# Issue order of the first loads, place of a query chunk, load slots, and the split of query transposes between DMA and PE

## The chip, the cores and the metric

The kernel runs on one core of a Trainium2 chip. The time is device microseconds (us) of that core, over several executions; the profile is of one of them. TensorE is PE, VectorE DVE, ScalarE ACT, GpSimd POOL, SyncE SP; PEclk is the share of PE's clock that was granted. On one core, slow is a run more than 1.5% above the fastest of the same kernel. A ratio's bracket is its 95% interval. Ratios are the mean time of one kernel's fast runs over that of the other's of the same rounds, so they are not quite the ratio of the medians that are quoted.

## The reference

Linear attention with cosine features, then a feed-forward network (FFN) with a product of two projections. Cut to what matters:

```python
def _attn_ref(q, k, v):                       # q, k, v: 8 batches x 8 heads x 576 x 64
    theta = np.pi / 2.0 * np.arange(S) / S
    phi = lambda x: concat([relu(x) * cos(theta), relu(x) * sin(theta)])   # 64 -> 128 features
    kv = einsum('bhsf,bhsd->bhfd', phi(k), v)
    z = sum(phi(k), axis=2)
    num = einsum('bhsf,bhfd->bhsd', phi(q), kv)
    den = einsum('bhsf,bhf->bhs', phi(q), z)[..., None] + 1e-06
    return num / den

def _moe_ref(x, w1, w2, w3, w_out):           # x: 4608 x 512, inner width 1024
    return (x @ w1) * (x @ w2) @ w3 @ w_out
```

Inputs and output are float32.

## The kernel before

W3 and w_out are multiplied into one matrix (w34b) at run time. The attention of a later batch is woven into the slots of each FFN tile, so that PE always has matmuls. The attention output (xblk) is turned into FFN input (xT) by PE for batch 0 and by DMA transposes from SP for all later batches. In the views, kf is the first keys in f32; ks, qs and vs are keys, queries and values in bf16; kp and qp are their features, qpT the turned query features and pst the buffer that PE turns them into; ffnps holds an FFN product and osb an output that is ready to be stored. Cuts are marked with dots:

```python
    load(0, "k", nc.sync)                     # first keys, f32, by SP's DMA queue
    load(0, "q")                              # bf16 (cast in the DMA), by GpSimd's queue
    ...
    idle_mms(32)                              # matmuls on zeros, before the keys land
    cosv, sinv = _trig_tables(nc, const)      # starts with two iotas on GpSimd
    identb = const.tile([P, P], BF16, name="identb")
    make_identity(nc, identb[:])
    ...
    load(0, "v")
    ...                                       # weights, then k, v, q of batch 1
    load(2, "kqv")

    def dma_q(b):                             # query chunks that a DMA turns, not PE
        return [] if b < 2 else order_of(b)[2:] if b < B - 1 else order_of(b)

    def features(dst, src, c):                # one chunk: cosine half on DVE, sine half on ACT
        ...

    def x_tr(b, c):                           # a chunk of attention output into xT, FFN's input
        ...
        if b >= 1:
            nc.sync.dma_start_transpose(out=xT[t][:, :, ds(o, R)], in_=xf)
            return
        ...                                   # batch 0: by PE, copied by ACT

    for t in range(NT):                       # nine FFN tiles of 512 rows, 24 slots each
        slots = [[] for _ in range(24)]
        if t == 0:
            ...
            attention_at(1, between, ..., nu=(12, 14, 16, 18, 20), xt=(12, 14, 16, 18, 20))
            ...
            slots[16].append(lambda: load(3, "kqv"))
            spread(prep_units(2), 17, 23, slots)
        else:
            if t + 3 < B:
                for g, name in ((0, "k"), (4, "q"), (8, "v")):
                    slots[g].append(lambda name=name: load(t + 3, name))
            ...
```

Of the kernel before, what the change touches and what calls it, by code (L numbers as in the profile page):

```python
# [19 lines left out]
NCH = 5  # L20
# [3 lines left out]
def _trig_tables(nc, pool):  # L24

    s_i = pool.tile([P, NCH], I32, name="s_i")
    nc.gpsimd.iota(s_i[0:64, :], pattern=[[1, 5]], base=0, channel_multiplier=5)
    nc.gpsimd.iota(s_i[64:128, :], pattern=[[1, 5]], base=320, channel_multiplier=4)
    th = pool.tile([P, NCH], FP32, name="th")
    nc.vector.tensor_copy(out=th[:], in_=s_i[:])  # L30
    nc.vector.tensor_scalar_mul(out=th[:], in0=th[:], scalar1=math.pi / 2 / S)
    t2 = pool.tile([P, NCH], FP32, name="t2")
    nc.vector.tensor_mul(out=t2[:], in0=th[:], in1=th[:])

    def poly(outt, coefs):
        nc.vector.tensor_scalar_mul(out=outt[:], in0=t2[:], scalar1=float(coefs[0]))
        for c in coefs[1:-1]:
            nc.vector.scalar_tensor_tensor(out=outt[:], in0=outt[:], scalar=float(c), in1=t2[:],
                                           op0=ALU.add, op1=ALU.mult)

    cosv = pool.tile([P, NCH], FP32, name="cosv")
    poly(cosv, [-1 / 3628800, 1 / 40320, -1 / 720, 1 / 24, -1 / 2, 1.0])
    nc.vector.tensor_scalar_add(out=cosv[:], in0=cosv[:], scalar1=1.0)
    sinv = pool.tile([P, NCH], FP32, name="sinv")
    poly(sinv, [-1 / 39916800, 1 / 362880, -1 / 5040, 1 / 120, -1 / 6, 1.0])
    nc.vector.scalar_tensor_tensor(out=sinv[:], in0=sinv[:], scalar=1.0, in1=th[:],
                                   op0=ALU.add, op1=ALU.mult)
    return cosv, sinv
# [3 lines left out]
def kernel(  # L52
# [12 lines left out]
    B = q.shape[0]  # L65
# [23 lines left out]
    def load(b, which, eng=nc.gpsimd):  # L89
        for name in which:  # L90
            src = {"k": k, "v": v, "q": q}[name]
            if eng is nc.gpsimd:
                t = ld.tile([P, H, NCH, D], BF16, name=name + "s")
            else:
                t = wst.tile([P, H, NCH, D], FP32, name=name + "f", bufs=1)
            eng.dma_start(out=t[0:64, :, :, :].rearrange("p h j d -> p h (j d)"),  # L96
                                in_=src[b, :, 0:320, :].rearrange("h (p j) d -> p h (j d)", j=5))
            eng.dma_start(out=t[64:128, :, 0:4, :].rearrange("p h j d -> p h (j d)"),
                                in_=src[b, :, 320:S, :].rearrange("h (p j) d -> p h (j d)", j=4))
            raw[b, name] = t  # L100
# [10 lines left out]
        nc.gpsimd.dma_start(out=w3b[:, jp, :], in_=moe_w3[ts(jp, P), :])  # L111

    load(0, "k", nc.sync)
    load(0, "q")
    zeros = const.tile([P, 512], BF16, name="zeros")
    nc.vector.memset(zeros[:], 0.0)
    tiny = const.tile([P, 1], FP32, name="tiny")
# [4 lines left out]
    def idle_mms(n):  # L122

        for _ in range(n):
            nc.tensor.matmul(unread[:, :], lhsT=zeros[:, 0:128], rhs=zeros[:], start=True, stop=True)

    idle_mms(32)
    cosv, sinv = _trig_tables(nc, const)
    identb = const.tile([P, P], BF16, name="identb")
    make_identity(nc, identb[:])  # L130
    va_bufs = []
    for i in range(2):
        va = const.tile([P, NCH, H, D + 2], BF16, name=f"va{i}")
# [42 lines left out]
    def order_of(b):  # L176

        return [0, 1, 2, 3, 4] if b % 2 == 0 else [4, 0, 1, 2, 3]

    def dma_q(b):  # L180

        return [] if b < 2 else order_of(b)[2:] if b < B - 1 else order_of(b)

    feat = {}

    def feat_of(b):
        if b not in feat:
            feat[b] = (
                phi.tile([P, NCH, H, F], BF16, name="kp"),
                phi.tile([P, NCH, H, F], BF16, name="qp"),  # L190
                va_bufs[b % 2],
            )
        return feat[b]
# [8 lines left out]
    def features(dst, src, c):  # L202
        R = ROWS[c]
        nc.vector.tensor_scalar(out=dst[:R, c, :, 0:D], in0=src[:R, :, c, :], scalar1=0.0,  # L204
                                scalar2=cosv[:R, c:c + 1], op0=ALU.max, op1=ALU.mult)
        nc.scalar.activation(out=dst[:R, c, :, D:F], in_=src[:R, :, c, :], func=ACTF.Relu,  # L206
                             scale=sinv[:R, c:c + 1], bias=0.0)

    def prep_k(b, c):
        features(feat_of(b)[0], raw[b, "k"], c)  # L210

    def prep_q(b, c):
        features(feat_of(b)[1], raw[b, "q"], c)
        if c in dma_q(b):
            R = ROWS[c]
            nc.sync.dma_start_transpose(out=att_of(b)["qpT"][:, :, ds(128 * c, R)],
                                        in_=feat[b][1][:R, c].rearrange("p h f -> p (h f)"))
# [42 lines left out]
    def q_tr(b, c, evac=True):  # L260
        R = ROWS[c]
        qp = feat[b][1]
        pst = ps_tr.tile([P, 8, 128], BF16, name="pst")
        for h in range(H):
            nc.tensor.transpose(pst[:, h, 0:R], qp[:R, c, h, :], identb[:R, :R])  # L265
        dst, src = att_of(b)["qpT"][:, :, ds(128 * c, R)], pst[:, :, 0:R]
        on_vector = lambda: nc.vector.tensor_copy(out=dst, in_=src)  # L267
        on_scalar = lambda: nc.scalar.copy(out=dst, in_=src)  # L268
        if evac:
            on_vector()  # L270
        return on_vector, on_scalar
# [22 lines left out]
    def x_tr(b, c):  # L294
        R = ROWS[c]
        xblk = att[b]["x"].pop(c)
        xf = xblk[:R].rearrange("p g h d -> p (g h d)")
        if b % 2 == 0:
            slot = S * b + 128 * c
        else:  # L300
            slot = S * b + (0 if c == 4 else 64 + 128 * c)
        t, o = divmod(slot, 512)
        if t not in xT:
            xT[t] = xtp.tile([P, 4, 512], BF16, name="xT")
# [3 lines that stand above are left out]
        pst = ps_tr.tile([P, 8, 128], BF16, name="pst")  # L308
        for kc in range(4):
            nc.tensor.transpose(pst[:, kc, 0:R], xf[:, ts(kc, 128)], identb[:R, :R])  # L310
        nc.scalar.copy(out=xT[t][:, :, ds(o, R)], in_=pst[:, 0:4, 0:R])
# [101 lines left out]

    for c in range(NCH):
        prep_k(0, c)
    for c in range(NCH):
        prep_q(0, c)
    q_tr(0, 0)
    q_tr(0, 1)
    idle_mms(1)  # L420
    for c in range(NCH):
        prep_v(0, c)
    for c in (2, 3):
        q_tr(0, c, evac=False)[1]()
    kv_first()
    idle_mms(1)
    num(0, 0)
# [10 lines left out]
    for t in range(NT):  # L438
        slots = [[] for _ in range(24)]
        if t == 0:  # L440
            slots[0].append(lambda: x_tr(0, 2))
            slots[1].append(lambda: x_tr(0, 3))
            slots[4].append(lambda: q_tr(0, 4))
            slots[7].append(lambda: num(0, 4))
            slots[9].append(lambda: x_tr(0, 4))
            slots[14].append(lambda: w3_tr(0))
            between = [[] for _ in range(32)]
            spread(prep_units(1, (prep_k,)), 2, 4, between)
            spread(prep_units(1, (prep_v,)), 5, 7, between)
            spread(prep_units(1, (prep_q,)), 8, 11, between)  # L450
            attention_at(1, between, kv=(7, 8, 8, 9, 9), tr=(10, 11, 13, 15, 17),
                         nu=(12, 14, 16, 18, 20), xt=(12, 14, 16, 18, 20))
            for jp in range(8):
                for part in range(2):
                    if part == 0 and jp < 7:
                        slots[15].append(lambda jp=jp: w3_tr(jp + 1))
                    slots[15].append(lambda jp=jp, part=part: w34_mm(jp, part))
                    slots[15] += between[2 * jp + part]
            for g in range(16, 24):
                slots[g] += between[g]  # L460
            slots[16].append(lambda: load(3, "kqv"))
            spread(prep_units(2), 17, 23, slots)
        else:
            if t + 3 < B:
                for g, name in ((0, "k"), (4, "q"), (8, "v")):
                    slots[g].append(lambda name=name: load(t + 3, name))
            if t + 1 < B:
                attention_at(t + 1, slots, kv=(0, 1, 2, 3, 4), tr=(2, 4, 7, 10, 13),
                             nu=(6, 8, 11, 14, 17), xt=(6, 8, 11, 14, 17))
            if t + 2 < B:  # L470
                each = [u for c in zip(*(prep_units(t + 2)[i:i + NCH] for i in (0, 5, 10))) for u in c]
                spread(each, 0, 22, slots)
        for g, _ in enumerate(ffn_groups(t)):
            for u in slots[g]:
                u()
# [30 lines left out]
```

## Time and profile before

| | before |
|---|---|
| median of the first three runs | 265.04 us (264.79 to 272.18, the last one slow) |
| span of the profiled run | 264.2 us |
| PE busy | 248.9 us, 94% |
| second keys land, first FFN matmul | 11.04 us, 24.20 us |
| FFN tile 1 starts, tile 2 starts | 69.75 us, 95.82 us |
| DMA transposes issued from SP | 55 (35 of xT, 20 of qpT) |

PE is nearly always busy, so a change helps only where it shortens PE's own work or removes one of its waits. The prediction below shows the lines from which I read that.

### The profile page before, as it was taken

What the parts mean: (1) busy time and instruction counts of PE and PEld (TensorE: products, weight loads), DVE (VectorE), ACT (ScalarE), POOL (GpSimd) and SP (SyncE); (2) the same over time, 40 slices, a digit from 0 to 9 for tenths busy, and PEclk for the clock granted to TensorE, in tenths of its full rate; (3) what the DMA queues carried; (4) which work ended last, traced back from release to release, by engine and by line L of the source; (5) the groups of instructions that cost most, each with busy time, mean ns of one, the idle gap of its engine ahead of it and who ended that gap; (6) DMA issues with size and microseconds to landing.
All of it is one profiled execution on the core that took longest, in us unless ns stands there. A gap on an engine that the chain in (4) does not pass through costs nothing.

```text
span 264.2 us, 4955 instructions
## 1 busy us (share of the span) xinstructions
PE 248.9 (94%) x1874; PEld 131.6 (50%) x1907; DVE 139.1 (53%) x334; ACT 125.6 (48%) x214; POOL 84.7 (32%) x143
## 2 busy tenths in 40 slices
PE   8478999999999989999999999999999999999993
PEld 3166545665464435445544545464445444444442
DVE  4366447567879616863883387278615723412320
ACT  2393435554955545555554565546543224333322
POOL 7552244331592275027504740430050022013000
PEclk9979999999999999999999999999999999999999
DMA  7999999999999999999997899744880334005014
GB/s 131 222 198 207 210 201 203 200 198 193 165 180 166 163 213 169 188 176 195 173 195 150 161 187 154 161 101 81 120 188 22 51 80 121 0 16 143 4 40 120
DMA packets 70600, 38.61 MB, mean 146 GB/s; under 512 B 38192, under 2 KB 67120, under 8 KB 70576
## 3 DMA queue, kind: packets, MB, share of 16 engines
q0 software_dynamic: 32400, 27.20, 63.2%
q1 hardware_dynamic: 38016, 10.95, 28.0%
q8 instruction: 15, 0.25, 0.4%
q10 hardware_dynamic: 160, 0.13, 0.2%
q14 instruction: 9, 0.07, 0.1%
HBM read 38.80 MB, written 9.44 MB: 183 GB/s over the span
## 4 chain that ended last, share of the span: by engine, by line
PE 85%; DMA 7%; ACT 3%; DVE 1%; issue 1%; SPq 0%; ACTq 0%
PE ffnps L353 47%; PE ffnps L382 20%; PE ffnps L170 5%; PE pnum L231 4%; DMA xT<-xblk 4%; PE pnum L281 4%; DMA kf<-in_k_dram 4%; PE pst L265 4%; PE pst L158 1%; ACT kp L206 1%; DVE xblk L288 1%; ACT qpT L268 1%; PE ffnps L399 0%; SPq L96 0%; ACT osb L401 0%
## 5 line engine op out<-in xcount | busy, mean ns | idle before, releaser
L377 DVE TENSOR_TENSOR abT<-asb,ffnps 128x512 bf16<-128x512 bf16 x70 | 47.9, 684 | 72.3 <-PE ffnps L353 71.2
L353 PE MATMUL ffnps<-xT,w1b 128*128 128x512 bf16 (+1 forms) x307 | 74.7, 362 | 2.3 <-DMA xT<-xblk 1.3
L353 PE MATMUL ffnps<-xT,w2b 128*128 128x512 bf16 (+1 forms) x296 | 73.2, 362 | 0.7
L373 ACT CAST asb<-ffnps 128x512 bf16<-128x512 f32 x70 | 40.9, 585 | 67.3 <-PE ffnps L353 61.7
L382 PE MATMUL ffnps<-w34b,abT 128*128 128x512 bf16 x273 | 63.2, 379 | 0.4
L345 POOL DMA_DIRECT2D out_dram<-osb x44 | 23.5, 540 | 121.9 <-ACT osb L388 121.8
L353 PEld LDWEIGHTS <-w1b 128*128 128x128 bf16 x312 | 27.9, 98 | 30.8 <-issue 3.0
L382 PEld LDWEIGHTS <-abT 128*128 128x128 bf16 x280 | 26.7, 98 | 30.6
L353 PEld LDWEIGHTS <-w2b 128*128 128x128 bf16 x312 | 26.8, 98 | 24.6
L388 ACT COPY osb<-ffnps 128x512 f32<-128x512 f32 x35 | 20.4, 584 | 38.6 <-PE ffnps L382 36.6
L206 ACT ACTIVATE qp<-qs,sinv 128x512 bf16<-128x512 bf16 (+1 forms) x40 | 28.0, 718 | 0.0
L288 DVE TENSOR_TENSOR xblk<-pnum,den 128x512 bf16<-128x512 f32 (+1 forms) x38 | 26.2, 689 | 1.5 <-DVE den L286 0.2
L206 ACT ACTIVATE kp<-ks,sinv 128x512 bf16<-128x512 bf16 (+1 forms) x35 | 24.5, 721 | 0.0
L281 PEld LDWEIGHTS <-qpT 128*128 128x128 bf16 (+1 forms) x320 | 14.9, 100 | 11.6 <-issue 3.6
L222 POOL COPY va<-vs 128x512 bf16<-128x512 bf16 (+1 forms) x30 | 18.8, 655 | 0.0
L265 PE MATMUL pst<-identb,qp 128*128 128x128 bf16 (+1 forms) x160 | 12.2, 226 | 5.3 <-ACT qp L206 5.3
L281 PE MATMUL pnum<-kvs,qpT 128*128 128x65 bf16 (+1 forms) x304 | 16.2, 194 | 0.0
L204 DVE TENSOR_SCALAR qp<-qs,cosv 128x512 bf16<-128x512 bf16 (+1 forms) x40 | 16.0, 418 | 0.0
L265 PEld LDWEIGHTS <-qp 128*128 128x128 bf16 (+1 forms) x160 | 10.4, 104 | 10.6 <-ACT qp L206 5.8
L231 PEld LDWEIGHTS <-kp 128*128 128x128 bf16 (+1 forms) x280 | 12.3, 97 | 6.6 <-issue 1.7
L170 PE MATMUL ffnps<-woutb,w3T 128*128 128x512 bf16 x60 | 15.2, 379 | 0.2
L267 DVE COPY qpT<-pst 128x1024 bf16<-128x1024 bf16 (+1 forms) x18 | 11.3, 630 | 7.4 <-PE pst L265 7.2
(64 smaller groups left out, 163.7 us busy)
## 6 DMA issues: line engine op xcount, KB each, us to landing
out_dram<-osb POOLq DMA_DIRECT2D x20, 256.0 KB, 3.9
out_dram<-osb POOLq DMA_DIRECT2D x24, 128.0 KB, 3.4
qs<-in_q_dram POOLq DMA_DIRECT2D x8, 320.0 KB, 9.2
vs<-in_v_dram POOLq DMA_DIRECT2D x8, 320.0 KB, 9.8
ks<-in_k_dram POOLq DMA_DIRECT2D x7, 320.0 KB, 10.2
qs<-in_q_dram POOLq DMA_DIRECT2D x8, 256.0 KB, 10.1
vs<-in_v_dram POOLq DMA_DIRECT2D x8, 256.0 KB, 10.5
w3b<-in_moe_w_dram POOLq DMA_DIRECT2D x8, 256.0 KB, 15.5
```

The source lines that it names most:

```text
L170: nc.tensor.matmul(acc[:, :], lhsT=w3T[:, lc, :], rhs=woutb[:, lc, :], start=(lc == 0), stop=(lc == 7))
L206: nc.scalar.activation(out=dst[:R, c, :, D:F], in_=src[:R, :, c, :], func=ACTF.Relu, scale=sinv[:R, c:c + 1], bias=0.0)
L231: nc.tensor.matmul(kvt[:, h // 4, ds((h % 4) * 65, 65)], lhsT=kp[:R, c, h, :], rhs=va[:R, c, h, 0:D + 1], start=(i == 0 and h % 4 == 0), s ...
L265: nc.tensor.transpose(pst[:, h, 0:R], qp[:R, c, h, :], identb[:R, :R])
L281: nc.tensor.matmul(nt[:R, h // 4, ds((h % 4) * 65, 65)], lhsT=qpT[:, h, ds(128 * c, R)], rhs=kvs[:, h, :], start=True, stop=True)
L288: nc.vector.tensor_tensor(out=xblk[:R], in0=n4[:, :, :, 0:D], in1=den[:R].unsqueeze(3).to_broadcast([R, 2, 4, D]), op=ALU.mult)
L345: on.dma_start(out=rows[:, :, cols], in_=osb[64 * i:64 * i + 64, :, cols])
L353: nc.tensor.matmul(out_ps[:, tok], lhsT=w[:, kc, ts(jc, 128)], rhs=x[:, kc, tok], start=(kc == 0), stop=(kc == 3))
L373: nc.scalar.copy(out=asb[:], in_=aT[:, :])
L377: nc.vector.tensor_mul(out=abT[:, jc, :], in0=asb[:], in1=bT[:, :])
L382: nc.tensor.matmul(ops[:, :], lhsT=abT[:, jc, ts(ms, 128)], rhs=w34b[:, jc, :], start=(jc == 0), stop=(jc == 7))
L388: nc.scalar.copy(out=osb[:, ms % 2, :], in_=ops[:, :])
```

## The change

The intent: give the first keys the DMA engines to themselves, take one chunk's work off the head, space the loads over a tile, and leave the DMA engines fewer query transposes in the tiles where loads are heavy.

```diff
--- before.py
+++ after.py
@@ -111,7 +111,6 @@
         nc.gpsimd.dma_start(out=w3b[:, jp, :], in_=moe_w3[ts(jp, P), :])
 
     load(0, "k", nc.sync)
-    load(0, "q")
     zeros = const.tile([P, 512], BF16, name="zeros")
     nc.vector.memset(zeros[:], 0.0)
     tiny = const.tile([P, 1], FP32, name="tiny")
@@ -124,10 +123,11 @@
         for _ in range(n):
             nc.tensor.matmul(unread[:, :], lhsT=zeros[:, 0:128], rhs=zeros[:], start=True, stop=True)
 
-    idle_mms(32)
+    idle_mms(36)
     cosv, sinv = _trig_tables(nc, const)
     identb = const.tile([P, P], BF16, name="identb")
     make_identity(nc, identb[:])
+    load(0, "q")
     va_bufs = []
     for i in range(2):
         va = const.tile([P, NCH, H, D + 2], BF16, name=f"va{i}")
@@ -179,7 +179,7 @@
 
     def dma_q(b):
 
-        return [] if b < 2 else order_of(b)[2:] if b < B - 1 else order_of(b)
+        return order_of(b)[5 if b < 3 else 3 if b == 3 else 2 if b < B - 1 else 0:]
 
     feat = {}
 
@@ -413,15 +413,15 @@
 
     for c in range(NCH):
         prep_k(0, c)
-    for c in range(NCH):
+    for c in range(4):
         prep_q(0, c)
     q_tr(0, 0)
     q_tr(0, 1)
     idle_mms(1)
     for c in range(NCH):
         prep_v(0, c)
-    for c in (2, 3):
-        q_tr(0, c, evac=False)[1]()
+    q_tr(0, 2)
+    q_tr(0, 3, evac=False)[1]()
     kv_first()
     idle_mms(1)
     num(0, 0)
@@ -440,6 +440,7 @@
         if t == 0:
             slots[0].append(lambda: x_tr(0, 2))
             slots[1].append(lambda: x_tr(0, 3))
+            slots[1].append(lambda: prep_q(0, 4))
             slots[4].append(lambda: q_tr(0, 4))
             slots[7].append(lambda: num(0, 4))
             slots[9].append(lambda: x_tr(0, 4))
@@ -462,7 +463,7 @@
             spread(prep_units(2), 17, 23, slots)
         else:
             if t + 3 < B:
-                for g, name in ((0, "k"), (4, "q"), (8, "v")):
+                for g, name in ((1, "k"), (8, "q"), (15, "v")):
                     slots[g].append(lambda name=name: load(t + 3, name))
             if t + 1 < B:
                 attention_at(t + 1, slots, kv=(0, 1, 2, 3, 4), tr=(2, 4, 7, 10, 13),
```

## The prediction

> **What bounds the kernel now.** I read four views in this order. First the page: TensorE (PE) is busy for 94% of a 264.2 us span, and of the chain that ended last 85% is PE and 7% is DMA. So the time is PE's work plus the few places where PE stands still. Second, the busy table in 40 slices (6.6 us each), to find those places and to see how full the DMA engines are:
>
> ```profile
> PE   8478999999999989999999999999999999999993
> PEclk9979999999999999999999999999999999999999
> DMA  7999999999999999999997899744880334005014
> ```
>
> PE has a hole in slices 1 to 3 (7 to 26 us) and a dent in slice 14 (92 to 99 us). The DMA engines are full from slice 1 on for 140 us. Third, PE's waits with the chain in order of time, to name both holes:
>
> ```profile
> PE pst L265 <- ACT qp L206: 5.3, 1, 5.3
> PE ffnps L353 <- DMA xT<-xblk: 1.3, 1, 1.3
> ...
> 1.56 9.47 DMA kf<-in_k_dram
> 11.39 0.38 issue
> 11.78 2.54 ACT kp L206 x4
> 14.32 0.62 ACT qp L206
> 14.99 1.89 PE pst L265 x16
> ...
> 85.89 9.69 DMA xT<-xblk
> ```
>
> The head hangs on the first keys: they land at 11.03 us, ScalarE (ACT) makes five key and five query feature chunks from 11.15 to 17.38 us, PE turns the queries, and the FFN begins at 24.20 us. The second hole is the start of FFN tile 2: PE stops at 94.5 us and waits to 95.8 for a DMA transpose issued at 85.89 that took 9.69 us. Fourth, the clock and the DMA queues in short stretches. In each row of the first two, the last three figures are granted clock, DMA share and GB/s:
>
> ```profile
> 15.00:16.00 1.00, 1.00 (x10) 1.00 (x11) 0.00 (x1) 1.00 (x2) 0.69 (x2) 0.50 1.44 196
> 17.00:18.00 1.00, 1.00 (x13) 0.90 (x12) 1.00 (x4) 0.38 (x1) 0.39 (x1) 0.67 1.45 196
> ...
> q1 hardware_dynamic: 219, 0.28, 95.9%
> ...
> q0 software_dynamic: 132, 0.08, 64.7%
> q1 hardware_dynamic: 100, 0.11, 64.7%
> ```
>
> The clock is at half from about 14.2 to 17.7 us. The keys' queue q1 moves 0.28 MB from 3 to 4 us, alone, and only 0.11 MB from 5 to 6 us, when the queries have joined on q0.
>
> [...] the keys fall from 0.28 to 0.11 MB a microsecond. [...] idle from 9.64 to 14.99 us, then half clock for some 3.4 us. [...] the trace shows GpSimd (POOL) in program order, idle only until ACT's osb copies or DMA landings. That matters for the spread loads.
>
> **The change part by part.**
>
> *First keys alone.* The two query loads (0.83 + 0.71 us on POOL) now come behind iota and identity (2.89 to 3.86 us, so 0.97 us). The queries start about 1 us later. In that microsecond the keys gain 0.28 - 0.11 to 0.17 = about 0.14 MB (0.17 is q1's rate from 8 to 9 us), and that many bytes cost them about 1 us at the shared rate. So keys land near 10.1 us. The queries should still land near 11.4, since the engines stay full and only the order of bytes changes; DVE first needs them at 10.1 + 2.2 = 12.3.
>
> *Four more idle matmuls.* 4 x 0.21 = 0.85 us, so PE is active until 10.5 instead of 9.64. The first query transposes would start near 10.1 + 3.8 = 13.9: a gap of 3.4 us instead of 5.3. [...] the clock should mostly stay full. In this trace the half clock made sixteen 128-column transposes take 1.89 us; at full rate eight take 0.45 in the later tiles.
>
> *Last query chunk later, third chunk's copy to DVE.* ACT loses one feature activation (0.63 us) and one 1.0 us copy before kvs: 1.6 us less. But the values' copies (1.08 us) and kv's 40 matmuls (1.75 us) follow, so not all counts. Working the order through from the landing, the first denominator comes at +9.0 instead of +9.7 us (20.86 - 11.15). The chunk's activation then sits on ACT between 27.2 and 27.8 us, where ACT idled 0.58 us: free. Head: 1.0 + 0.7 = 1.7 us, or 1.1 to 1.2 against an execution of before whose clock happened to stay full. I take 1.4.
>
> *Four query chunks from DMA to PE.* The slice now leaves batch 2 no DMA chunk (three before) and batch 3 two (three before); 55 transposes become 51. PE gets 32 transposes: three full chunks at 0.44 us each (72.85 to 73.29) and one of 64 rows at 0.34 (99.22 to 99.56) = 1.66 us, all on a full PE. DVE gets four copies, 3 x 0.69 + 0.42 = 2.5 us; it was busy 17.3 of 25 us in tile 1, so they fit. In return SyncE issues nothing for 7.54 us (70.25 on) nor for 2.18 us at 83.61:
>
> ```profile
> 70.25 7.54 SPq L216 DMA_TRANSPOSE qpT<-qp  x3
> 79.78 3.44 SPq L306 DMA_TRANSPOSE xT<-xblk  x2
> 83.61 2.18 SPq L216 DMA_TRANSPOSE qpT<-qp  x1
> 85.89 5.56 SPq L306 DMA_TRANSPOSE xT<-xblk  x2
> ```
>
> The late xT chunk had its source at 85.0 (DVE ends at 84.31 + 0.69), stood behind the query chunk until 85.89 and queued behind four such transposes. Without them I expect it in 5 to 7 us, before PE needs it; the 1.3 us wait goes.
>
> *Loads spread over the tile.* The slots order only the program. In tile 1, POOL issued keys, queries and values between 74.3 and 79.5 us back to back with copies, because nothing there waits for PE. In the changed order each of queries and values moves behind one more copy of about 0.63 us. That is no spreading. I give it 0.
>
> *Sum without collision:* -1.4 - 1.3 + 1.66 = -1.0 us.
>
> **The collision, and other rivals.** (a) *The gain of the head is lost at tile 1.* The last xT chunk that tile 1 needs, issued at 66.60, took 3.0 us, so landed at 69.6; PE begins tile 1 at 69.75:
>
> ```profile
> 66.60 1.46 SPq L306 DMA_TRANSPOSE xT<-xblk  x1
> ...
> 69.75 1.02 PE ffnps L353 x4
> ```
>
> The margin is 0.1 us. The chunk one before took 5.3 us, since the loads of batches 1 to 3 fill the DMA engines until about 68. Nothing in the change takes bytes off the engines before 70 us, so a PE that comes 1.4 us earlier could find its xT not there. Against it: the xT transposes are issued earlier too [...]. If everything lands as before, the 1.4 us are all given back: 265.04 + 0.36 = 265.4. I expect half. (b) *The tile 2 wait stays*, as the new loads still crowd the same window: +1 us, 265. For it speaks that DMA shows nines from 80 to 91 us; against it, four transposes of up to 2.8 us of issue each are gone. (c) *DVE becomes late in tile 1*, with 19.1 of 25 us and both transpose buffers in play; each late copy stalls PE some tenths, +0.5. (d) *More comes off*: the keys, alone, land at 9.5 and tile 1 finds its xT: 262.8.
>
> **Range and chances.** -1.0 without collision, and +0.7 for half of (a). Against that I set -0.4, a guess and no reading: with less DMA work after 70 us some of the 0.2 to 0.3 us by which PE's busy time falls short in each of the windows 24 to 39, 39 to 66 and 69 to 94 us may close. Together -0.7: about 264.3 us. The ends come from the rivals: 262.8 if (d) comes and the clock stays full, 265.6 if (a) takes all and (c) adds a little. 2% is 5.3 us; the two waits touched sum to 6.6 us, and most of the 5.3 before the queries cannot go, so faster by over 2% has 1 in 100. Slower by over 2% needs a wait of several microseconds that nothing here points to: 2 in 100.
>
> **What would show it.** In the changed profile: first key feature at about 10.2 us (11.15 now), granted clock 1.0 from 11 to 18 us, first FFN matmul near 22.7 (24.20 now); the wait for xT at tile 2 gone, perhaps a new one of up to 1 us near 69; 192 query transposes on PE where the program has 160 now; POOL's loads still in one burst of about 6 us. I am wrong in the head if the keys land no earlier, wrong in the sum if tile 1 starts at 69.6 again, and wrong altogether if PE shows a new wait for DVE's copies.

The sum came to -1.4 - 1.3 + 1.66 = -1.0 us without collision, and with +0.7 and -0.4 to about 264.3 us. That a gap of 3.4 us leaves the clock full was my estimate, not shown. The trace had one case: half clock from 14.24 to 17.66 us, which set in 4.6 us into a wait of 5.3 us. Of the 1.7 us for the head, 0.5 to 0.6 hung on a full clock (1.7 less 1.1 to 1.2).

## The result, and the profile after

The median after is 273.15 us (271.64 to 274.06, four runs). Against the kernel before, whose median was 265.21 us in the same comparison, the ratio is 1.0299, with a 95% interval of 1.024 to 1.0359: slower by over 2%, which I had given 2 in 100, and far outside my range of 262.8 to 265.6. The span of the profiled run is 269.8 us, 5.6 us over before. The same three rows of the busy table (40 slices, now of 6.7 us):

```profile
PE   8799999999499999999999999999999999999990
PEclk9999999999799999999999999999999999999997
DMA  6999999999999179977996899836680162023033
```

The hole at the start is nearly gone, and the dent of slice 14 too. A new, deeper dent is in slice 10 (67 to 74 us), with a granted clock of 0.7, while DMA shows nines up to there. PE's waits of the changed kernel (total, times, longest) name it:

```profile
PE ffnps L353 <- DMA xT<-xblk: 3.9, 1, 3.9
PE pst L265 <- ACT qp L206: 1.8, 1, 1.8
```

The chain in order of time (start, duration, what) shows both ends of the story:

```profile
1.56 7.95 DMA kf<-in_k_dram
...
64.31 6.92 DMA xT<-xblk
71.37 1.87 PE ffnps L353 x4
...
262.64 2.96 ACTq L345
```

The keys land at 1.56 + 7.95 = 9.51 us, 1.5 us earlier. The first FFN matmul starts at 21.92 us instead of 24.20: the head gains 2.28 us. But the last xT chunk that tile 1 needs, issued 2.3 us earlier than before (64.31 for 66.60), lands at 71.2, 1.6 us later than before (69.6). PE has been idle since 67.43. And the four matmuls after the wait take 1.87 us where four took 1.02 at 69.75 us in the kernel before. The table in short stretches says why; the last three figures are granted clock, DMA share and GB/s:

```profile
70.00:71.00 1.00, 0.00 (x0) 0.00 (x0) 0.00 (x0) 0.00 (x0) 1.00 (x3) 1.00 0.92 360
72.00:73.00 1.00, 1.00 (x3) 0.30 (x2) 0.00 (x0) 0.00 (x0) 1.00 (x2) 0.50 0.91 287
```

The clock falls to half just as the work comes back, and stays there from 71.22 to 74.64 us. In the last line of the chain, ACT takes 2.96 us to issue its first store of the last tile; the kernel before needed 0.56 us (ACT's timeline):

```profile
259.13 0.56 ACTq L345 DMA_DIRECT2D out_dram<-osb  x1
```

So the two profiles differ as follows. Tile starts are those of PE's timeline; each row is what the stretch added.

| stretch | before | after | added |
|---|---|---|---|
| start to first FFN matmul | 24.20 | 21.92 | -2.28 |
| first FFN matmul to tile 1 | 45.55 | 49.45 | +3.90 |
| tile 1 to tile 2 | 26.07 | 27.51 | +1.44 |
| tile 2 to start of last tile (238.66; 242.18) | 142.84 | 143.30 | +0.46 |
| last tile to the end | 25.5 | 27.6 | +2.1 |
| span | 264.2 | 269.8 | +5.6 |

The second row is the wait for xT. In the third, 1.3 us of wait went and 0.44 + 0.44 + 0.34 = 1.22 us of transposes came, which leaves about 1.5 us; I put it to the clock, and run 4 tests that. The fourth is the one transposed chunk of batch 3. The last is ACT's store. The timed runs differ by more, 7.9 us in their medians; a second profile of the same kernel (below) shows a clock that stays down for two stretches.

### The profile page after: what moved, and what is told of

Read it like the earlier page. It is cut to its first block, busy times and chain, and to the rows that moved or that the text cites. A ratio compares the mean times of both kernels' runs of the same rounds, so it can differ in the third digit from the quotient of the medians.

```text
span 269.8 us, 5049 instructions
## 1 busy us (share of the span) xinstructions
PE 255.2 (95%) x1943; PEld 133.5 (49%) x1943; DVE 142.3 (53%) x339; ACT 125.0 (46%) x213; POOL 83.8 (31%) x143
## 4 chain that ended last, share of the span: by engine, by line
PE 84%; DMA 8%; ACT 2%; DVE 2%; ACTq 1%; issue 1%; SPq 0%
PE ffnps L353 47%; PE ffnps L382 20%; PE ffnps L170 4%; PE pnum L231 4%; PE pst L265 3%; PE pnum L281 3%; DMA kf<-in_k_dram 3%; DMA qs<-in_q_dram 3%; DMA xT<-xblk 3%; PE pst L158 1%; ACTq L345 1%; ACT kp L206 1%; DVE xblk L288 1%; ACT qp L206 0%; DVE kp L204 0%
## 5 line engine op out<-in xcount | busy, mean ns | idle before, releaser
L353 PE MATMUL ffnps<-xT,w1b 128*128 128x512 bf16 (+1 forms) x312 | 75.8, 366 | 4.5 <-DMA xT<-xblk 3.9
L353 PE MATMUL ffnps<-xT,w2b 128*128 128x512 bf16 (+1 forms) x312 | 75.6, 365 | 0.0
L267 DVE COPY qpT<-pst 128x1024 bf16<-128x1024 bf16 (+1 forms) x23 | 14.4, 630 | 6.8 <-PE pst L265 6.2
L204 DVE TENSOR_SCALAR qp<-qs,cosv 128x512 bf16<-128x512 bf16 (+1 forms) x40 | 17.1, 443 | 0.3 <-DMA qs<-in_q_dram 0.3
L170 PE MATMUL ffnps<-woutb,w3T 128*128 128x512 bf16 x64 | 15.8, 379 | 0.0
L265 PEld LDWEIGHTS <-qp 128*128 128x128 bf16 (+1 forms) x192 | 11.3, 97 | 8.4 <-ACT qp L206 2.4
L265 PE MATMUL pst<-identb,qp 128*128 128x128 bf16 (+1 forms) x192 | 13.6, 213 | 1.8 <-ACT qp L206 1.8
```

Source lines behind the costliest of these rows:

```text
L170: nc.tensor.matmul(acc[:, :], lhsT=w3T[:, lc, :], rhs=woutb[:, lc, :], start=(lc == 0), stop=(lc == 7))
L265: nc.tensor.transpose(pst[:, h, 0:R], qp[:R, c, h, :], identb[:R, :R])
L353: nc.tensor.matmul(out_ps[:, tok], lhsT=w[:, kc, ts(jc, 128)], rhs=x[:, kc, tok], start=(kc == 0), stop=(kc == 3))
```

## The experiments

Theory 1: the faster head brings PE to tile 1 before the DMA engines have worked off the loads of batches 1 to 3; PE waits there for xT, and its clock halves. Theory 2, the rival: the slice of query chunks (more transposes on PE, more copies on DVE) is what costs. Theory 3 came up on the way: ACT's slow store depends on its place in ACT's program. The first eight runs were on one chip, the last four on another. The kernel before ran beside them: its median was 266.91 us beside runs 1 to 4, 266.6 beside 5 to 8 and 264.98 beside 9 to 12, so a run is judged by its ratio and not against 265.21.

**1. The head put back** (queries first, 32 idle matmuls, all five query chunks in the head):

```diff
     load(0, "k", nc.sync)
+    load(0, "q")
 ...
-    idle_mms(36)
+    idle_mms(32)
 ...
-    load(0, "q")
 ...
-    for c in range(4):
+    for c in range(NCH):
         prep_q(0, c)
 ...
-    q_tr(0, 2)
-    q_tr(0, 3, evac=False)[1]()
+    for c in (2, 3):
+        q_tr(0, c, evac=False)[1]()
 ...
-            slots[1].append(lambda: prep_q(0, 4))
```

> The changed kernel with its whole head put back (queries issued first, 32 idle matmuls, fifth query chunk and the third chunk's copy where they were); slice and load slots stay changed. Theory 1 (the faster head brings PE to tile 1 before the DMA engines have drained, so PE waits 3.9 us for xT there and the clock halves): PE arrives at tile 1 near 69.7 again, waits under 0.5 us, the clock stays full after the head, the time is 264.5 to 266.5. Theory 2 (the slice, four chunks more on PE and fewer on DMA, is what slows the kernel): the loss stays, 270 us or more.

Measured: 266.06 us, ratio 0.9985 (0.9913 to 1.0058). The first FFN matmul is at 24.88 us and PE waits little at tile 1, as its waits show:

```profile
PE ffnps L353 <- DMA xT<-xblk: 0.4, 1, 0.4
```

The slice and the slots alone are thus neither gain nor loss that these rounds can see. Theory 2 falls: the loss belongs to the head.

**2. The slice put back:**

```diff
-        return order_of(b)[5 if b < 3 else 3 if b == 3 else 2 if b < B - 1 else 0:]
+        return [] if b < 2 else order_of(b)[2:] if b < B - 1 else order_of(b)
```

> The changed kernel with the old slice of query chunks by DMA (three for batches 2 to 6). Theory 1: the wait of about 3.9 us at tile 1 and the half clock after it stay, since the slice moves nothing before 70 us; the time is 270.5 to 273.5, at most 1.7 us less than the changed kernel for the 32 transposes, less any wait that comes back at tile 2. Theory 2: back to 264 to 267 us.

Measured: 269.47 us, ratio 1.0109 (1.0046 to 1.0172), still above before, and the same wait in PE's list, longer still:

```profile
PE ffnps L353 <- DMA xT<-xblk: 5.3, 1, 5.3
```

The wait does not need the slice. The time is 1 us under my range. ACT's store took 0.56 us here, 2.4 us less than in the changed kernel, and that made me look at the store.

**3. The values of batch 3 loaded after tile 0's stores:**

```diff
-            slots[16].append(lambda: load(3, "kqv"))
+            slots[16].append(lambda: load(3, "kq"))
 ...
         else:
+            if t == 1:
+                slots[0].append(lambda: load(3, "v"))
             if t + 3 < B:
```

> The changed kernel with the values of batch 3 loaded after the stores of tile 0 instead of before them: 0.59 MB less, near 3 us of DMA at 0.2 MB/us, ahead of the xT transposes of tile 1. Theory 1: the last xT of tile 1 lands near 68.3 instead of 71.2, the wait shrinks from 3.9 to 1 us or less, the clock stays full there (1.7 us more), the time is 266 to 268.5 us. Theory 2: no change, 271 to 274 us. A new wait for these values at tile 2 is possible and would show as PE waiting for kv matmuls near 97 us.

Measured: 266.26 us (266.18 to 266.66), ratio 0.9997. The last xT of tile 1 lands at 67.46, PE's list has no wait for xT at all, and the clock is full from 7 us to the end of the work. Taking two transfers out from ahead of the transposes removes both wait and half clock. The feared wait at tile 2 did not come. ACT's store still took 2.83 us.

**4. Ten idle matmuls between tile 0 and tile 1:**

```diff
+        if t == 1:
+            fill = ps_ffn.tile([P, 512], FP32, name="ffnps")
+            for _ in range(10):
+                nc.tensor.matmul(fill[:, :], lhsT=zeros[:, 0:128], rhs=zeros[:], start=True, stop=True)
         for g, _ in enumerate(ffn_groups(t)):
```

> The changed kernel with ten idle matmuls (10 x 0.216 = 2.2 us) on PE between tile 0 and tile 1. They take no data from the wait, only its idleness. Theory 1 with the half clock as a part of the loss: tile 1 starts at the same 71.3, but no stretch of half clock follows, and the time is 1.5 to 1.9 us under the changed kernel, 270 to 272. If the clock plays no part: no change within 0.5 us.

Measured: 270.35 us, ratio 1.0157 (1.0082 to 1.0233). The idle wait shrinks to 2.6 us, tile 1 starts no earlier (72.11), and the clock stays full, in the same short stretches:

```profile
70.00:71.00 1.00, 0.00 (x0) 0.00 (x0) 0.00 (x0) 0.00 (x0) 1.00 (x3) 1.00 0.84 326
72.00:73.00 1.00, 0.83 (x4) 0.44 (x6) 0.00 (x0) 0.00 (x0) 1.00 (x2) 1.00 1.08 407
```

Tile 1 then takes 98.06 - 72.11 = 25.95 us instead of 27.51. So the half clock cost 1.56 us in the profile of the changed kernel.

**5. As 3, with two more one-column activations at ACT's start:**

```diff
-    nc.scalar.activation(out=tiny[:], in_=zeros[:, 0:1], func=ACTF.Relu, scale=1.0, bias=0.0)
+    for _ in range(3):
+        nc.scalar.activation(out=tiny[:], in_=zeros[:, 0:1], func=ACTF.Relu, scale=1.0, bias=0.0)
```

> The run with the values of batch 3 loaded later, plus two more one-column activations on ACT at its very start, where it is idle. In three runs so far (the changed kernel, values later, fill) ACT's first store at the end took 2.8 to 3.0 us to issue, and ACT's trace has 327 entries; in three others (before, head undone, slice undone) it took 0.56 us, with 328 to 330 entries. Theory 3: this is [...] because of where the store stands in ACT's program; two entries more move it off and the tail shortens by 2.3 us: 263.7 to 264.6 us, under the kernel before. Rival: the long issue comes from the traffic or the state of the chip at the end, then it stays at 2.8 us and the time at 266 to 266.7.

Measured: 263.83 us (263.68 to 264.59, six runs), 2.4 us under run 3 and a ratio of 0.9907 (0.9855 to 0.9959) to the kernel before. ACT's timeline has its store short again:

```profile
257.38 0.56 ACTq L346 DMA_DIRECT2D out_dram<-osb  x1
```

PE's timeline shows tile 1 beginning where PE arrives, with no wait marked (in the profile of the changed kernel the line at 71.37 carries one of 3.94):

```profile
67.68 1.02 PE L354 MATMUL ffnps<-xT,w1b 128*128 128x512 bf16 x4
```

This version is 0.4 to 1.5% under the kernel before, clear of noise though less than 2%.

**6. The changed kernel with only the two activations** (the diff of run 5):

> The changed kernel with only the two more activations. Theory 3: ACT's last store issues in 0.56 us, the time falls by 2.3 us, to 269.5 to 271.8, while the wait for xT at tile 1 stays at 3.9 to 5.3 us with its half clock. Rival: 271.6 to 274 as before.

Measured: 271.11 us (267.45 to 271.58), ratio 1.0131 (1.0008 to 1.0254). The store took 0.56 us, and the wait for xT was 5.0 us. The profiled run counts as slow here, only because one run was at 267.45, so I take no size from it. The two faults are separate: this cures the tail and leaves the wait.

**7. The kernel before with the values of batch 3 later** (the diff of run 3 on the kernel before):

> The kernel before with the values of batch 3 loaded after the stores of tile 0. If the late loads are what limits tile 1 only once PE comes early (theory 1), this changes little at tile 1, where PE had 0.1 us of margin: tile 1 starts at 69.6 to 69.8; tile 2's wait of 1.3 us may grow, since the values then join the crowded window: 265 to 267 us. If the postponed load is a gain of its own, independent of the head: 262 to 264.

Measured: 269.4 us, ratio 1.0075 (0.9966 to 1.0184), above my range. At tile 1 nothing is gained (70.23). Tile 2 waits more, as PE's timeline shows:

```profile
97.48 1.27 PE L353 MATMUL ffnps<-xT,w1b 128*128 128x512 bf16 x4 [2.48 <-DMA xT<-xblk]
```

The clock halved after this wait too (98.12 to 101.54 us), and for two stretches in the head. Moving the values shows no gain of its own; with the fast head (run 3) it took the wait away.

**8. Values later, fast head, old slice** (the diffs of runs 3 and 2):

> Fast head, values of batch 3 later, and the old slice of query chunks by DMA. It asks what the slice is worth once the collision at tile 1 is gone. If the slice is worth it: tile 2 waits for xT again, by 2 us or more (1.3 in the kernel before plus the later values), and the time is above the padded version, 265 to 267 us. If the slice only costs its 1.66 us of transposes: 262.5 to 263.5 us. ACT's last store should issue in 0.56 us, as its program has two entries more than the changed kernel's.

Measured: 265.85 us (262.57 to 271.13), two of four runs slow; ratio 0.9892 (0.9776 to 1.0008), unclear. The two fast runs are 262.57 and 264.5, on either side of run 5. In the profile, a slow run, PE did not wait at tile 2 (it starts at 93.10 us), so the old slice need not bring that wait back; it waited 2.1 us for xT at tile 3, and the clock halved there (120.75 to 124.17 us). What the slice is worth without the collision is not settled: the runs without it spread over 8.6 us, those with it over 0.9 us (run 5).

**9. The changed kernel again, on the second chip:**

> The changed kernel once more, unaltered, on the chip and in the rounds of the others, so that they can be set against it. Theory 1 and 3: 271 to 274 us, ACT's last store 2.8 to 3.0 us to issue, a wait of 3.5 to 5.5 us for xT at tile 1, half clock [...] after it.

Measured: 273.06 us, ratio 1.0313 (1.0284 to 1.0341). Wait 4.1 us, store 2.84 us. The clock was down for two stretches, 70.25 to 77.08 us; one row of the short stretches:

```profile
76.00:77.00 1.00, 1.00 (x4) 0.35 (x3) 0.47 (x2) 0.00 (x0) 1.00 (x3) 0.50 1.38 183
```

Tile 1 took 100.07 - 71.42 = 28.65 us, 2.70 us over run 4. That would explain why the timed runs lie above the first profile: they were granted 0.981 to 0.983 of the clock, against 0.986 there.

**10. On the kernel before, only the queries behind and 36 idle matmuls:**

```diff
     load(0, "k", nc.sync)
-    load(0, "q")
 ...
-    idle_mms(32)
+    idle_mms(36)
 ...
     make_identity(nc, identb[:])
+    load(0, "q")
```

> The kernel before with only the first queries issued behind iota and identity and 36 idle matmuls; chunk order, slice and load slots as before. It splits the head. From the landing of the keys (11.0 to 9.5 us in the two traces) this part alone should bring the first FFN matmul from 24.2 to about 22.7; the rest of the 2.28 us is the chunk order. Theory 1: PE then reaches tile 1 near 68.2, finds its xT not landed before 69.6 to 71, and waits 1.5 to 3 us; time 265 to 268 us, no gain over before. If the wait belonged to the chunk order instead: no wait at tile 1 and 263.5 us.

Measured: 266.75 us, ratio 1.0076 (1.0031 to 1.0121). The first FFN matmul is at 21.94 us, against 21.92 with the chunk order changed too, so this part alone makes the head's gain; the chunk order adds nothing that shows in these two profiles. The wait came with it, in PE's timeline:

```profile
72.38 1.86 PE L353 MATMUL ffnps<-xT,w1b 128*128 128x512 bf16 x4 [4.92 <-DMA xT<-xblk]
```

A step that is right for the head, put into the old kernel alone, makes the whole 0.3 to 1.2% slower.

**11. As 5, with the old load slots:**

```diff
-                for g, name in ((1, "k"), (8, "q"), (15, "v")):
+                for g, name in ((0, "k"), (4, "q"), (8, "v")):
```

> The best version so far (fast head, new slice, values of batch 3 later, two more activations) with the load slots of before (0, 4, 8 for 1, 8, 15). By the order of GpSimd's program the slots move queries and values by one copy of 0.63 us each and nothing more: within 0.5 us of 263.8. If the spread matters for the transposes in the middle tiles: 265 or more.

Measured: 263.86 us (263.66 to 264.03), ratio 0.9961 (0.9947 to 0.9974); run 5 had 263.83 on the other chip, with a ratio of 0.9907 (0.9855 to 0.9959). The slots do nothing that shows across the two chips.

**12. The two activations, and two xT chunks of batch 1 turned by PE:**

```diff
-        if b >= 1:
+        if b >= 1 and not (b == 1 and c in (1, 2)):
 ...
-                         nu=(12, 14, 16, 18, 20), xt=(12, 14, 16, 18, 20))
+                         nu=(12, 14, 16, 18, 20), xt=(12, 14, 18, 20, 20))
```

> The changed kernel plus two more activations, with the two xT chunks of batch 1 that tile 1 waited for turned by PE and copied by ACT, at slots 18 and 20; all loads stay where they are. Theory 1: with no xT left behind the loads, tile 1 starts at 67.9 (0.45 us of transposes more) to 69 us (ACT is full there and may copy late), no half clock, and the time is 264 to 266 us. If something else than these transposes held tile 1, it still starts after 71.

Measured: 264.23 us (264.03 to 265.54), ratio 0.9986 (0.9962 to 1.001). All loads stay ahead, and tile 1 starts when PE gets there:

```profile
66.40 2.75 PE L383 MATMUL ffnps<-w34b,abT 128*128 128x512 bf16 x12
68.99 1.03 PE L354 MATMUL ffnps<-xT,w1b 128*128 128x512 bf16 x4
```

In this profiled run the head's clock was at half from 14.89 to 18.30 us, so PE arrived later than in run 5. Runs 3 and 12 take away the same wait from its two sides, the loads ahead and the transposes behind them.

## Why the prediction was wrong

**Keys.** Right in direction, small in size: 1.5 us earlier, not 1.0. The keys' queue from 5 to 6 us, where before it shared with q0:

```profile
q1 hardware_dynamic: 181, 0.19, 110.4%
```

q0 is not in that answer at all. Its first packets came between 7 and 8 us; before, between 4 and 5. I had moved them by the 0.97 us of work in front, and POOL in fact issued only 0.59 us later (1.87 for 1.28); from issue to first packet it took 5.7 us for 3.6, and no run says why. The queries landed at 11.84, not 11.36. I had said that the engines stay full and only the order of bytes changes. That was wrong: by 10 us the same 1.18 MB of keys had gone, but q0 had moved less (first the kernel before, then the changed one):

```profile
q0 software_dynamic: 909, 0.52, 37.6%
q0 software_dynamic: 620, 0.38, 26.5%
```

The 0.15 MB are still missing at 60 us (10.41 for 10.56 MB on q0), which is 0.75 us at q0's own 0.2 MB/us (0.20 MB in each microsecond from 9 to 13 us of the changed kernel). All eleven profiles with the queries behind have 0.34 to 0.39 MB on q0 by 10 us, the three others 0.52.

**Idle matmuls.** In the profile the clock stayed full, as I said, but after a gap of 1.8 us and not the 3.4 that I had estimated. And runs 8 and 12 had the same 36 and half clock in the head, after gaps of only 2.6 and 2.7 us, so four more do not secure it. Their first FFN matmul came at 23.14 and 23.20 us: by these profiles, about 1.2 us of the head's gain hangs on the clock.

**Chunk order.** I gave 0.7 us to it and to the full clock together. Run 10 has the same head without the chunk order (21.94 us for 21.92): nothing of its part shows.

**Head.** 1.4 us predicted, 2.28 measured.

**Slice.** 1.66 us of transposes on PE and the end of the 1.3 us wait: both seen (192 query transposes, no wait at tile 2). Run 1, which keeps slice and slots on the old head, agrees with my +0.36 within its interval, which is wide (-2.3 to +1.5 us).

**Other rivals.** (b) and (c) did not come: PE's list has no wait at tile 2 and none for DVE's copies in tile 1. Of (d) the first half came, keys at 9.5 us; tile 1 did not find its xT.

**Slots.** Right. POOL's timeline of the changed kernel shows one burst, with 2.5 and 1.9 us from name to name:

```profile
71.91 0.70 POOL L96 DMA_DIRECT2D ks<-in_k_dram  x1
...
74.42 0.68 POOL L96 DMA_DIRECT2D qs<-in_q_dram  x1
...
76.31 0.68 POOL L96 DMA_DIRECT2D vs<-in_v_dram  x1
```

**The step that failed** is the size of rival (a): "If everything lands as before, the 1.4 us are all given back: 265.04 + 0.36 = 265.4. I expect half." I had named the place, the chunk and the 0.1 us of margin, and then took the old landing of 69.6 as the worst case. Three things exceed that.

First, the xT landed later than before, at 71.24, although it was issued 2.3 us earlier: the last load issued before it drained at 70.33 instead of 68.96. I had read the full DMA engines as a fixed amount of work that ends at a fixed time; it ended 1.4 us later. By my estimate 0.75 us of that are the bytes that the head left behind (**Keys**). Nor does the earlier issue put xT in front of the loads, for those come earlier with it. I had written that POOL idles only until osb copies or landings; before 66 us it also waits for ACT's features, and it issued the queries of batch 3 2.3 us earlier, too (before, then changed):

```profile
57.15 0.68 POOL L96 DMA_DIRECT2D qs<-in_q_dram  x1 [6.61 <-ACT qp L206]
54.86 0.68 POOL L96 DMA_DIRECT2D qs<-in_q_dram  x1 [4.01 <-ACT qp L206]
```

The wait was therefore 3.9 us, 5.3 in run 2. Second, I did not price the clock after the wait: 1.56 us (run 4), or 2.70 us when it stays at half for 6.83 us (run 9). I had counted the half clock that came with the head's wait (14.24 to 17.66 us) and none after the wait that I was predicting. Third, 2.1 us at the tail, which no view of the kernel before could show. The guess of -0.4 for closing small gaps had nothing behind it, and nothing of it was seen.

With the three put in as measured, the terms add up to what the profile shows: -2.28 + 3.90 - 1.3 + 1.66 + 1.5 + 2.1 = 5.6 us.

**What is shown and what is argued.** Shown: the loss comes with the head (runs 1 and 10), through xT behind loads (runs 3 and 12), with the clock as a part (4) and the store as a part (5). ACT's trace had 327 entries in each of the four profiles with a slow store (changed kernel, runs 3, 4, 9) and 328 to 331 in the ten others, all at 0.55 or 0.56 us. The place in ACT's program is thus shown to matter (runs 5 and 6). What makes the place matter is not shown. The profiles show only a coincidence in time: an 8 KB packet on q14, which the page lists as an instruction queue, starts 1.2 to 1.3 us into each of the four slow issues (263.92 in the changed kernel), and 1.5 to 1.6 us ahead of each of the ten short ones (257.59 in the kernel before). Open: the rest of the 1.4 us by which the loads drained later, some 0.6 us. The second keys of batch 3 land 0.78 us later (62.28 for 61.50), before any xT has landed; the rest arises while transposes, loads and stores share the engines, and no run took that apart.

## What to carry to other kernels

When one stage is made faster, look up for every input of the next stage when it lands and what that landing depends on. Here it hung on DMA engines that were full up to there (nines in the busy table): the stage waited there for 3.9 us, and the change that made it arrive earlier delayed the landing, from 69.6 to 71.2 us. Price the wait with its consequence, the half clock afterwards (1.56 us by run 4, 2.70 us in run 9). The length of the wait alone did not decide it: a wait of 2.1 us was followed by half clock (run 8), one of 2.6 us after ten idle matmuls by full clock (run 4). Take the work ahead of the critical transfer off the queue first (a load that can come later, as in run 3, or a transpose that PE can do, as in run 12), and only then speed up what comes before it.
